# Attention, then a SwiGLU block by fast matrix products: the first block's output product in two passes of two terms each, its last two weight conversions after its up products

## The chip, the cores and the metric

The kernel runs on one core of a Trainium2 chip. The metric is the device time of one execution in microseconds (us), the median of several runs. Engines are named as in the profile: PE (matrix products; PEld is its weight load), DVE (vector engine), ACT (scalar engine), POOL (GpSimd), SP (the queue that issues most transfers).

## The reference

```python
# q, k, v: (8, 12, 448, 64); g_q, g_k: (64,); w_gate, w_val: (768, 1536); w_out: (1536, 768)
def rmsnorm(x, g):
    return x / np.sqrt(np.mean(x * x, axis=-1, keepdims=True) + 1e-06) * g
scores = 1 / np.sqrt(64) * rmsnorm(q, g_q) @ rmsnorm(k, g_k).transpose(0, 1, 3, 2)
attn = softmax(scores)                                 # over the keys
x = (attn @ v).transpose(0, 2, 1, 3).reshape(3584, 768)
g = x @ w_gate
out = (g / (1 + np.exp(-g)) * (x @ w_val)) @ w_out     # (3584, 768)
```

The weights come as 64-bit floating point numbers, everything else as 32-bit ones.

## The kernel before, in words

`general` is a slow version that runs only if a test on `g_q` and `g_k` fails; everything below is `fast`.

**Stages.** Twelve heads make six pairs of heads for each of eight batches, 48 pairs `m`. Two batches make a block of 896 tokens; there are four blocks. The first 12 pairs (`EARLY`) run first. Then, for each block, come its up products (gate and value) and its output products; the 12 pairs of the next block run between the output products.

**Products.** Every matrix product is cut into 3x3 blocks and done with 15 products of sums of blocks. The token sums (`sides`, line 1055) are made on DVE from six raw blocks and stand in `xs` in 15 slots, two of 448 columns each. Up products (`up_product`, L1328) go through four groups `g` of 128 hidden columns, 15 steps, gate and value, two matmuls each, in four banks; a bank is read after each product by ACT (a copy) or DVE (an add or subtract, lines 1272 to 1276). The results, gated, stand in `gt`, six parts of four groups. From them DVE makes token sums again (`combine`, L1454; `combined`, L1049 and L1053), and the output products (`down_product`, L1502) go through 15 steps and two halves `s`. Each adds up four matmuls, one for each group `g`, in bank `s`, which is read before the next step writes it (`DOWN_READ`).

**Weights.** `convert` (L1120) makes 24 sets of weight sums: five transfers load 9 blocks of 64-bit numbers, two ACT instructions, six DVE instructions (shift, sign, round; L1168, L1174, L1180) and twelve POOL instructions (L1199, L1202) follow, and one transfer stores 15 block sums in DRAM, in `up_sides[g]` (16 sets) or `down_sides` (8 sets). `load_sides` brings them back into one of two `ws` buffers, three loads for each group of up products, eight for an output product. The conversions work in places that belong to other tiles: parts of `gt` (`GT`), `hs` (`HS`), the tile of exponentials (`ES`), the slots of `xs` from 6 on (`XS`), the pairs' work tile (`PAIRS`) and `spare` (`SPARE`). `staged[place]` is the last store out of a place; loads of pairs wait for `PAIRS`, scores for `ES`.

**Order.** `Order` (L361) plans all instructions by itself: each piece has a due time `when`, a `rank` that makes it more urgent, a cost in us, what it waits for, and tiles that it takes from rings. At each step it picks, over all engines, the piece that can start earliest, and among those near to each other the one with the smallest `when - rank`. What it emits is the order of each engine's queue. Reads of up banks have rank 60, reads of output banks 20, conversions 20 from the seventh set on. The due times of the conversions are `starts` and `spans`, their places `turns`, at the end of `fast`.

Of the kernel before, what the change touches and what calls it, by code (L numbers as in the profile page):

```python
# [477 lines left out]
def fast(  # L478
# [87 lines left out]
    def take(name, key, shape):  # L566
# [4 lines left out]
        if name in OFTEN:  # L571
            at = OFTEN[name] + order.turn[name] % BUFS[name]
            tiles[name, key] = spare[:, ts(at, S)]
            return tiles[name, key]
        if name == "eh":
            at = order.turn["eh"] % BUFS["eh"]
            tiles[name, key] = more[:, at].rearrange("p (h q) -> p h q", h=2)
            return tiles[name, key]
# [35 lines left out]
    down_sides = dram.tile([P, 15, 2, NG, P], F32, name="down_sides")  # L614
# [88 lines left out]
    def attention(m):  # L703
# [306 lines left out]
        def divide():  # L1010
# [4 lines left out]
            "ACT", 0.55, when + 3.0, copy_sums, after=[last, up_done.get(b // 2 - 1)], uses=at[:1]  # L1015
# [39 lines left out]
    def sides(n, c, when):  # L1055
# [7 lines left out]
        for i, one, two, op in (  # L1063
# [15 lines left out]
            if n == 0:  # L1079
                free = [staged[place] for place in XS]  # L1080
# [39 lines left out]
    def convert(key, src, sums, to, when, place, by_bank):  # L1120

        rank = 20.0 if by_bank else 0.0
# [7 lines left out]
        wait = [last_exp[0]] if place in (ES, PAIRS, GT[2]) else []  # L1130
# [110 lines left out]
    def down_weights(i, *how):  # L1241

        g, s = divmod(i, 2)
        w = moe_w_out.rearrange("(k g p) (n s f) -> p k g n s f", g=NG, p=P, n=3, s=2)
        weights["down", i] = convert(
            ("down", i), lambda k, n: w[:, k, g, n, s], DOWN_SUMS, down_sides[:, :, s, g], *how
        )
# [3 lines left out]
    down_done = {}  # L1251
    last_load = []
# [25 lines left out]
    def load_sides(key, sides, part, sums):  # L1278

        size = 2 * (NC2 if sums is UP_SUMS else NG) * P  # L1280
        to = take(*key, [P, WS])[:, 0 : len(part) * size].rearrange("p (x f) -> p x f", f=size)
        i = 0
        for names, first in ((sums, 0), (BLOCKS, len(sums))):
            here = sorted(names.index(x) for x in part if x in names)
            if here:
                size = len(here)
                src = sides[:, ds(first + here[0], size)]
                nc.sync.dma_start(to[:, ds(i, size)], src.rearrange("p x a b f -> p x (a b f)"))
                i += size
# [5 lines left out]
    def block(n):  # L1295
# [123 lines left out]
        def up_load(g, piece):  # L1419
# [3 lines left out]
                lambda: load_sides(key, up_sides[g], UP_ORDER[5 * piece :][:5], UP_SUMS),  # L1423
# [6 lines left out]
        for g in range(NG):  # L1430
# [5 lines left out]
        up_done[n] = last  # L1436
        bank_read[:] = [free[0, 0], free[0, 1]]
# [3 lines left out]
        raw = [gt[:, :, k] for k in range(6)]  # L1441
        a1, a2, a3, b1, b2, b3 = raw
        h0, h1 = hs[:, 0], hs[:, 1]
# [3 lines left out]
            6: h0, 1: h1, 10: h2, 14: b1, 2: h0, 3: h1, 0: a3, 11: h2, 4: b3, 12: h0, 5: a1, 8: h1,  # L1447
            7: b2, 13: b1, 9: a2,
        }
        all_hidden = [hidden[g, k] for g in range(NG) for k in range(6)]  # L1450
# [3 lines left out]
        def combine(x, one, two, op, when, after, g=None):  # L1454
            to = where[x]
            if g is not None:
                to, one, two = to[:, g], one[:, g], two[:, g]
            done = add(
                "DVE", 0.64 if g is not None else 2.05, when,
                lambda: combined(to, one, two, op), after=after, port=True,  # L1460
            )
            made.setdefault(x, []).append(done)
            return done

        span = (BOTH if n < NB - 1 else DOWN) / 15

        def step_time(x):
            return block_end(n) + DOWN_ORDER.index(x) * span

        for g in range(NG):  # L1470
            when = start + 30 * (g + 1) * unit + 1.0
            before = [down_done.get(n - 1)] + ([staged[HS]] if n == 0 else [])
            combine(6, a1, a2, None, when, [hidden[g, 0], hidden[g, 1], *before], g)
            combine(1, b2, h0, ALU.subtract, when, [made[6][g], hidden[g, 4], *before], g)
        combine(10, h1, b1, None, block_end(n) + 3.0, [*all_hidden, *made[1], up_done[n]])
# [5 lines left out]
        def down_product(step, x, s):  # L1481
            nonlocal last
            when = step_time(x) + s * span / 2
            piece = step // 2
            key = ("ws", (n, "o", piece))
            size = 2 if piece < 7 else 1
            if piece not in loads:
                loads[piece] = add(
                    "SP", 0.9, when - 24.0,
                    lambda: load_sides(key, down_sides, DOWN_ORDER[2 * piece :][:2], DOWN_SUMS),  # L1490
                    after=[*last_load, *(weights["down", i] for i in range(2 * NG))], takes=[key],
                    kb=512 * size, early=10.0,
                )
                last_load[:] = [loads[piece]]
            fresh = x in FRESH

            def emit():
                w = tiles[key][:, 0 : 4 * NG * P]
                w = w.rearrange("p (x s g f) -> p x s g f", s=2, g=NG, f=P)
                at = place_of(x, DOWN_ORDER[step - step % 2 :][:2], DOWN_SUMS)  # L1500
                for g in range(NG):
                    nc.tensor.matmul(  # L1502
                        banks[s][:, 0:S], w[:, at, s, g], where[x][:, g],
                        start=fresh and g == 0, stop=g == NG - 1, skip_group_check=True,
# [3 lines left out]
                "PE", 2 * PRODUCT, when, emit,  # L1508
                after=[
                    last, loads[piece], bank_read[s], *made.get(x, []),  # L1510
# [5 lines left out]
            when += 2 * PRODUCT  # L1516
            t, how, *final = DOWN_READ[x]
            name = "vw"[s] + {"t0": "0", "t1": "1", "t4": "2", "t3": "3", "d": "3", "t5": "4"}[t]
            value = (name, (n, "o", t))
# [15 lines left out]
            if x == 12:  # L1535
                other = ("vw"[s] + "1", (n, "o", "t1"))
# [7 lines left out]
            if not final:  # L1544
# [25 lines left out]
        for step, x in enumerate(DOWN_ORDER):  # L1570
            when = step_time(x)
            for s in range(2):
                down_product(step, x, s)
            after = {
                6: [(2, b3, b1, ALU.subtract, (1,))],
                1: [(3, h0, a3, ALU.add, (2, 10))],
                10: [(11, a3, b3, ALU.add, ()), (4, b2, b3, None, (2, 11))],
                14: [(13, a2, b2, ALU.add, (2, 10))],
                2: [(12, h1, a1, ALU.subtract, (3,))],
                3: [(8, a3, b2, ALU.subtract, (12,)), (9, a2, a3, ALU.add, (6, 13))],  # L1580
            }.get(x, [])
            for to, one, two, op, others in after:
                combine(
                    to, one, two, op, when + span,
                    [*all_hidden, *products[n, x], *(d for o in others for d in made[o])],
                )
# [28 lines left out]
    turns = [(*XS, *GT[:2], HS, SPARE), (ES, PAIRS, GT[2], SPARE, HS), (ES, PAIRS, HS, SPARE), (ES, HS)]  # L1615
    starts = [LEAD - 4.0, FIRST - 20.0, FIRST + 60.0, FIRST + 110.0]
# [81 lines left out]
```

## Time and profile before

| | us |
|---|---|
| median of 3 runs | 1486.81 (1485.77 to 1488.26) |
| profiled execution | 1485.77 |
| its span, first to last instruction | 1484.0 |
| PE busy | 1425.0 |
| DVE busy | 916.0 |
| ACT busy | 681.5 |
| POOL busy | 414.1 |

Stretches of the span, cut where PE goes from one kind of product to the next: first pairs until 141.7; up products of block 0 until 329.7; its output products with pairs 12 to 23 until 505.1; up products of block 1 until 690.6; its output products until 855.3; and so on, with the last output products from 1386.4 on.

The profile is one execution as the hardware recorded it. A matmul stands as two records, so a 128x448 one in groups of x4 is two matmuls. In a timeline, a row is start, length, engine, line, operation, output and input; the bracket at its end is idle time of the engine ahead of it and what ended it. A list of waits has who waited for whom, then us in total, times, and the longest. Idle time of an engine that is off the path costs nothing. The granted PE clock was 0.997 of full speed over the span.

### The profile page before, as it was taken

The numbers are of one execution on the slowest core, as the hardware profiler recorded it, in microseconds if no ns is written. First come the engines' busy times: TensorE is split into PE (matmuls) and PEld (weight loads), VectorE is DVE, ScalarE is ACT, GpSimd is POOL, SyncE is SP. The second block draws the span as 40 slices with busy tenths as digits, with TensorE's granted clock in tenths as the row PEclk, the third lists the DMA queues.
The fourth block names the chain that finished last, engine by engine and source line by source line (L and its number), as shares of the span: only waits on it lengthen the run. The fifth ranks groups of instructions, "written<-read, shape, count | busy, mean of one in ns | idle before, by whom it ended". The sixth has DMA issues, their size and how long they took to land.

```text
span 1484.0 us, 19470 instructions
## 1 busy us (share of the span) xinstructions
PE 1425.0 (96%) x6672; PEld 675.4 (46%) x6672; DVE 916.0 (62%) x1405; ACT 681.5 (46%) x1366; POOL 414.1 (28%) x468
## 2 busy tenths in 40 slices
PE   5789999999999999999999999999999999999998
PEld 2334544443444455544444445554444445555553
DVE  4777887877978544355886733454786854432533
ACT  6774544437775322445767422354676532122100
POOL 2454586636444100012544200011343410000000
PEclk9999999999999999999999999999999999999999
DMA  7767999974453432533344432352353442222235
GB/s 165 158 144 236 292 308 341 296 219 90 99 115 85 113 106 71 138 103 90 74 111 110 100 117 73 106 136 77 96 119 85 90 119 89 80 98 73 83 98 107
DMA packets 415921, 193.30 MB, mean 130 GB/s; under 512 B 324164, under 2 KB 397892, under 8 KB 409668
## 3 DMA queue, kind: packets, MB, share of 16 engines
q1 hardware_dynamic: 402688, 190.35, 48.0%
q10 hardware_dynamic: 12996, 1.61, 0.7%
q8 instruction: 55, 0.90, 0.3%
q14 instruction: 54, 0.44, 0.1%
q0 software_dynamic: 128, 0.00, 0.0%
HBM read 157.29 MB, written 34.60 MB: 129 GB/s over the span
## 4 chain that ended last, share of the span: by engine, by line
PE 73%; DVE 3%; ACT 2%; issue 1%; DMA 1%; SPq 1%; ACTq 0%; DVEq 0%
PE mm L1502 22%; PE mm L1328 20%; PE at L1328 20%; PE st L840 6%; PE at L916 5%; PE st L947 1%; ACT spare L1000 1%; ACT es L855 1%; DVE rd L982 1%; DMA out_dram<-spare 0%; SPq L728 0%; DVE ss L782 0%; DMA work<-in_k_dram 0%; DVE ss L768 0%; DVE sums L866 0%
## 5 line engine op out<-in xcount | busy, mean ns | idle before, releaser
L1328 PE MATMUL mm<-xs,ws 128*128 128x448 f32 x960 | 401.2, 540 | 4.4 <-DVE spare L1276 2.2
L1328 PE MATMUL at<-xs,ws 128*128 128x448 f32 x960 | 400.6, 540 | 4.1 <-DVE v L1274 2.6
L1328 PEld LDWEIGHTS mm<-xs,ws 128*128 128x128 f32 x960 | 181.5, 190 | 185.8 <-issue 173.8
L1328 PEld LDWEIGHTS at<-xs,ws 128*128 128x128 f32 x960 | 181.9, 190 | 184.6 <-issue 172.6
L795 POOL TENSOR_TENSOR work<-work,rr 128x448 f32<-128x448 f32 x96 | 105.9, 1122 | 503.5 <-DVE rr L686 245.2
L840 PE MATMUL st<-work 64*64 64x448 f32 (+1 forms) x1536 | 155.1, 508 | 27.3 <-ACT work L814 21.2
L1502 PE MATMUL mm<-gt,ws 128*128 128x448 f32 x448 | 177.2, 545 | 0.0
L1272 DVE TENSOR_TENSOR gt<-gt,mm 128x448 f32<-128x448 f32 x64 | 39.7, 621 | 185.1 <-PE mm L1328 171.3
L1502 PE MATMUL mm<-hs,ws 128*128 128x448 f32 x384 | 152.1, 545 | 0.9 <-DVE ss L684 0.9
L855 ACT ACTIVATE es<-st 128x896 f32<-128x896 f32 x129 | 114.3, 913 | 56.1 <-PE at L916 42.8
L860 POOL TENSOR_TENSOR sums<-es 128x896 f32<-128x896 f32 x36 | 75.7, 2104 | 195.8 <-PE st L947 83.2
L1402 ACT ACTIVATE st<-gt 128x448 f32<-128x448 f32 x96 | 52.4, 547 | 163.8 <-DVE gt L1276 85.9
L1000 ACT COPY spare<-rd 32x224 f32<-32x224 f32 x288 | 108.1, 375 | 35.0 <-DVE rd L982 30.7
L1502 PEld LDWEIGHTS mm<-gt,ws 128*128 128x128 f32 x448 | 82.9, 190 | 84.2 <-issue 81.0
L916 PE MATMUL at<-es,v 64*64 64x448 f32 x1032 | 110.2, 545 | 7.2 <-ACT xs L1005 3.3
L1270 ACT COPY gt<-mm 128x448 f32<-128x448 f32 x80 | 42.5, 531 | 141.5 <-PE mm L1328 141.4
L1502 PEld LDWEIGHTS mm<-hs,ws 128*128 128x128 f32 x384 | 71.1, 190 | 72.9 <-issue 70.9
L840 PEld LDWEIGHTS st<-work 64*64 64x64 f32 x1536 | 50.9, 134 | 108.7 <-issue 38.1
L1270 ACT COPY v<-at 128x448 f32<-128x448 f32 x96 | 51.1, 532 | 83.2 <-PE at L1328 80.0
L860 POOL TENSOR_TENSOR sums<-sums,es 128x896 f32<-128x896 f32 x36 | 78.7, 2187 | 2.8
L811 DVE STREAM_TRANSPOSE work<-work 128x448 f32<-128x448 f32 x96 | 59.2, 627 | 25.2 <-POOL work L795 23.1
L916 PEld LDWEIGHTS at<-es,v 64*64 64x64 f32 x1032 | 39.7, 134 | 67.4 <-issue 57.4
(150 smaller groups left out, 1568.7 us busy)
## 6 DMA issues: line engine op xcount, KB each, us to landing
ws<-up_sides SPq DMA_DIRECT2D x32, 1024.0 KB, 4.9
ws<-down_sides SPq DMA_DIRECT2D x16, 1024.0 KB, 5.0
ws<-down_sides SPq DMA_DIRECT2D x28, 512.0 KB, 4.0
ws<-up_sides SPq DMA_DIRECT2D x16, 768.0 KB, 4.6
work<-in_q_dram SPq DMA_DIRECT2D x192, 56.0 KB, 2.4
work<-in_k_dram SPq DMA_DIRECT2D x188, 56.0 KB, 2.5
out_dram<-spare SPq DMA_DIRECT2D x168, 56.0 KB, 1.9
v<-in_v_dram SPq DMA_DIRECT2D x96, 96.0 KB, 2.5
```

The costliest lines, as they stand in the source:

```text
L795: nc.gpsimd.tensor_tensor(out=tiles["t", m][:, x], in0=tiles["qk", (m, x)], in1=rr.to_broadcast([P, NC, C]), op=ALU.mult,)
L811: nc.vector.transpose(to, tiles["t", m][:, x].rearrange("p c f -> p (c f)"))
L840: nc.tensor.matmul(st[ds(D * x, D), h, 0:n], tiles["KT", m][rows, ds(P * j + D * of_keys, D)], tiles["QT", m][rows, ds(Q * of_queries, n)] ...
L855: nc.scalar.activation(e, tiles["st", (m, j)][:, :, 0 : S * width(j) // P], AF.Exp)
L860: nc.gpsimd.tensor_tensor(out=to, in0=tiles["e", (m, 0)] if j == 1 else to, in1=e, op=ALU.add)
L916: nc.tensor.matmul(tiles["at", (m, x)][ds(D * h, D), queries], tiles["v", m][rows, j, h], tiles["e", (m, j)][rows, h], start=j == 0, stop= ...
L1000: nc.scalar.copy(inv[ds(D * h + C * to, C), ts(x, Q)], tiles["rd", m][ds(D * h + C * x, C)])
L1270: nc.scalar.copy(to, ps)
L1272: nc.vector.tensor_tensor(out=to, in0=old, in1=ps, op=ALU.add)
L1328: nc.tensor.matmul(ps(), w[:, at, which, c], xs[:, SLOT[x], c], start=fresh and c == 0, stop=c == NC2 - 1, skip_group_check=True,)
L1402: nc.scalar.activation(take(*act, [P, 2, TB])[:, 0, 0:S], to, AF.Silu)
L1502: nc.tensor.matmul(banks[s][:, 0:S], w[:, at, s, g], where[x][:, g], start=fresh and g == 0, stop=g == NG - 1, skip_group_check=True,)
```

## The change

- Block 0's output product runs in two passes. The first takes groups `g` 0 and 1 of all 15 steps, the second groups 2 and 3; each product has two matmuls. Every bank is read once in each pass; in the second pass, values that the first copied are added to or subtracted from, except `d`, whose value of the first pass is kept in a tile of its own (`v5` and `w5`, the latter in a raw slot of `xs`) and subtracted at the end. Sums (`combine`) are made for each pass, half as wide; they follow `BEHIND` and `readers` in place of written lists of waits.
- `down_sides` is two tensors, one for each pair of groups, and a pass's loads wait for its own four conversions; in block 0 a load brings four steps, not two.
- The last two of the 24 conversions go to `XS`, due at the end of the up products and after the last of them. Of the six before, places change: `ES, PAIRS, SPARE, HS, SPARE, HS` in place of `ES, PAIRS, HS, SPARE, ES, PAIRS`.
- All conversions have rank 0.
- Token sums of block 1 wait for the conversions in `XS`, and the copy of pair 23's sums waits for the last use of `w5`.

Other blocks keep one pass. The diff, cut:

```diff
+        if name == "w5":
+            tiles[name, key] = xs[:, SLOT[RAW[1][2]], 1]
+            return tiles[name, key]
...
-    down_sides = dram.tile([P, 15, 2, NG, P], F32, name="down_sides")
+    down_sides = [dram.tile([P, 15, 2, 2, P], F32, name=f"down_sides{i}") for i in range(NG // 2)]
...
-            "ACT", 0.55, when + 3.0, copy_sums, after=[last, up_done.get(b // 2 - 1)], uses=at[:1]
+            "ACT", 0.55, when + 3.0, copy_sums, uses=at[:1],
+            after=[last, up_done.get(b // 2 - 1), *(c3_used if m == 2 * EARLY - 1 else [])],
...
-            if n == 0:
-                free = [staged[place] for place in XS]
+            if n < 2:
+                free = [*free, *(staged[place] for place in XS)]
...
-    def convert(key, src, sums, to, when, place, by_bank):
-        rank = 20.0 if by_bank else 0.0
+    def convert(key, src, sums, to, when, place, by_bank, wait=()):
+        rank = 0.0 if by_bank else 0.0
...
-        wait = [last_exp[0]] if place in (ES, PAIRS, GT[2]) else []
+        wait = [*wait, *([last_exp[0]] if place in (ES, PAIRS, GT[2]) else [])]
...
+        if n == 0:
+            for make, index, when, place in late_weights:
+                make(index, when, place, True, [last])
...
+        passes = [(0, 2), (2, 4)] if n == 0 else [(0, NG)]
...
+        BEHIND = {6: (2,), 1: (3,), 10: (11, 4), 14: (13,), 2: (12,), 3: (8, 9)}
...
-        def combine(x, one, two, op, when, after, g=None):
-            to = where[x]
+        def combine(p, x, when, after, g=None):
+            one, two, op = SUMS[x]
+            names, (to, *values) = zip(*(place(p, i) for i in (x, one, two)))
...
+            us = 0.3 + 0.44 * (passes[p][1] - passes[p][0])
+            if g is None:
+                after += readers.pop(names[0], [])
...
+            many = 4 if n == 0 else 2
+            piece = step // many
...
-                    after=[*last_load, *(weights["down", i] for i in range(2 * NG))], takes=[key],
-                    kb=512 * size, early=10.0,
+                    after=[
+                        *last_load, *(weights["down", g, i] for g in range(lo, hi) for i in range(2))
+                    ],
+                    takes=[key], kb=128 * len(part) * (hi - lo), early=10.0,
...
-                for g in range(NG):
+                for g in range(hi - lo):
...
-                "PE", 2 * PRODUCT, when, emit,
+                "PE", 2 * PRODUCT / len(passes), when, emit,
...
+            sums_too = p and t != "d"
...
+            if split and not p and t == "d":
+                name = "5"
+            value = ("vw"[s] + name, (n, "o", t, 0 if sums_too else p))
+            if sums_too and how == COPY:
+                how = ADD if t in ("t1", "t3") else FROM
...
+                if p:
+                    c3 = ("vw"[s] + "5", (n, "o", "d", 0))
+                    drained[s, "d"] = add(
+                        "DVE", 0.64, when + 1.5,
+                        lambda: nc.vector.tensor_tensor(
+                            out=tiles[value], in0=tiles[value], in1=tiles[c3], op=ALU.subtract
+                        ),
+                        after=[drained[s, "d"]], uses=[value, c3], port=True,
+                    )
+                    c3_used.append(drained[s, "d"])
-            if not final:
+            if not final or p < len(passes) - 1:
                 return
...
+        for p in range(len(passes)):
+            for step, x in enumerate(DOWN_ORDER):
+                for s in range(2):
+                    down_product(p, step, x, s)
+                for other in BEHIND.get(x, ()):
+                    combine(p, other, step_time(p, x) + span, all_hidden)
+                if x == 9 and p < len(passes) - 1:
+                    combine(p + 1, 10, step_time(p, x) + span, all_hidden)
...
-    turns = [(*XS, *GT[:2], HS, SPARE), (ES, PAIRS, GT[2], SPARE, HS), (ES, PAIRS, HS, SPARE), (ES, HS)]
-    starts = [LEAD - 4.0, FIRST - 20.0, FIRST + 60.0, FIRST + 110.0]
-    spans = [13.0, 8.0, 9.0, 10.0]
+    turns = [(*XS, *GT[:2], HS, SPARE), (ES, PAIRS, GT[2], SPARE, HS), (ES, PAIRS, SPARE, HS, SPARE, HS), XS]
+    starts = [LEAD - 4.0, FIRST - 20.0, FIRST + 60.0, block_end(0)]
+    spans = [13.0, 8.0, 9.0, 12.0]
     counts = [6, 10, 6, 2]
...
-            make(index, starts[n] + spans[n] * i, turns[n][i % len(turns[n])], n > 0)
+            when, place = starts[n] + spans[n] * i, turns[n][i % len(turns[n])]
+            if n < 3:
+                make(index, when, place, n > 0)
+            else:
+                late_weights.append((make, index, when, place))
```

## Prediction

> **What bounds the kernel now.** I read the page's busy shares first: PE works 96% of the span, so only idle PE time or work added to PE moves the end. Then busy time by stage, cut where PE passes from one kind of product to the other: up products of block 0, its output products with the second dozen of attention pairs, up products of block 1, output products of blocks 1 and 2.
>
> ```profile
> PE 1425.0 (96%) x6672; PEld 675.4 (46%) x6672; DVE 916.0 (62%) x1405; ACT 681.5 (46%) x1366; POOL 414.1 (28%) x468
> ...
> 141.70:329.70 188.00, 182.28 (x482) 91.10 (x483) 152.37 (x228) 83.19 (x113) 111.84 (x216) 1.00 0.95 293
> 329.70:505.06 175.36, 170.03 (x1105) 71.68 (x1104) 139.10 (x205) 117.74 (x273) 81.27 (x48) 1.00 0.46 102
> 505.06:690.60 185.54, 185.54 (x529) 92.79 (x530) 82.15 (x145) 64.11 (x122) 11.93 (x10) 1.00 0.36 102
> 690.60:855.30 164.70, 162.00 (x1056) 71.65 (x1054) 124.70 (x176) 105.35 (x234) 65.00 (x38) 1.00 0.45 100
> ```
>
> Columns: stretch, length, then busy time of PE, PEld, DVE, ACT and POOL. Block 0 is the exception: its up stage takes 188.0 us though it holds fewer PE instructions than block 1's (185.5 us), and its output stage 175.4 against 164.7. Next, whom PE waits for in block 0's up stage, and PE and DVE in order of time around the longest of these waits:
>
> ```profile
> PE at L1328 <- DVE v L1274: 2.6, 2, 1.5
> PE at L1328 <- DVE v L1272: 1.2, 1, 1.2
> PE mm L1328 <- DMA ws<-up_sides: 0.9, 2, 0.6
> ```
>
> ```profile
> 237.06 1.67 PE L1328 MATMUL mm<-xs,ws 128*128 128x448 f32 x4
> 240.27 1.77 PE L1328 MATMUL at<-xs,ws 128*128 128x448 f32 x4 [1.55 <-DVE v L1274]
> ```
>
> ```profile
> 234.79 0.76 DVE L1168 TENSOR_SCALAR st<-es 128x576 uint32<-128x576 uint32 x1
> 235.64 0.78 DVE L1174 SCALAR_TENSOR_TENSOR st<-es,st 128x576 uint32<-128x576 uint32 x1
> 236.55 0.76 DVE L1180 CUSTOM_DVE_ANT_0 es<-es,st 128x1152 uint16<-128x1152 uint16 x1
> 237.34 0.76 DVE L1168 TENSOR_SCALAR st<-es 128x576 uint32<-128x576 uint32 x1
> 238.14 0.76 DVE L1174 SCALAR_TENSOR_TENSOR st<-es,st 128x576 uint32<-128x576 uint32 x1
> 238.93 0.75 DVE L1180 CUSTOM_DVE_ANT_0 es<-es,st 128x1152 uint16<-128x1152 uint16 x1
> 239.61 0.61 DVE L1274 TENSOR_TENSOR v<-v,at 128x448 f32<-128x448 f32 x1
> ```
>
> The six DVE instructions of one weight conversion stand in a row, 4.8 us, and the bank read behind them comes too late for PE. Other rows of the two timelines show the same run ahead of the waits at 231.9, 268.8, 280.2 and 289.0.
>
> **The PE unit prices.** An up product (four records) starts 1.504 us after the one before; an output product in full is twice that, 3.008. From groups of x16: a 64x448 matmul 0.188, a 64x224 one 0.096. A change of array mode: in block 1's up stage, scores of 1.14 us put between two products move the next one by 1.39 (658.50 to 659.89) and the one after by 0.11 more, 0.35 for two changes, 0.17 each. By these prices the up stage of block 1 is 185.3 (it took 185.5), so they hold.
>
> **Block 0, up stage: removes 6.1 us, takes over 5.5.** From start to start, the five waits on DVE cost 0.66+1.81+1.43+0.92+1.29 = 6.1 (each wait, and 0.1 on the product behind it); the two on `ws` 1.4. In the changed kernel two of the eight output-weight conversions leave this stage, and the rest lose 20 us of rank. I laid its DVE order against its PE order: adding DVE durations between reads, each read due before the fourth product from it starts. For the kernel before this finds four waits, at the products of the last four rows (2.3, 1.1, 0.6, 1.4); for the changed one none, also with all DVE work 10% dearer. So 6.1 goes. The `ws` waits I leave: a lower rank may make stored weights later (up to some 3 us), fewer transfers (DMA share 0.95 here) may remove the 1.4. What comes in: scores of the first pairs, whose places are free earlier, 16 matmuls 64x448 and 8 of 64x224 (3.8 us), with 10 mode changes (1.7). Net -0.6.
>
> **Block 0, output stage: work.** Matmuls are the same 120; pieces are halved, so attention is cut into finer slices: 52 mode changes become 69, +2.9; the moved scores take 3.8 away. Work by prices 167.2 before, 166.4 after: -0.9.
>
> **Block 0, output stage: lost time.** 175.4 - 167.2 = 8.1 before; block 1's has 164.7 - 161.8 = 2.9. The 5.2 between are mostly waits in its first 30 us (PE is idle 3.5 of 330 to 360), where attention starts from nothing because the pairs' and exponentials' tiles were held by conversions until 296 and 316. The changed order starts attention in the up stage as block 1 does, so I take 2.9 as the base. Against that stands DVE. Between the first full sum and the last turned output of block 0 its queue, by durations of this trace, grows from 142.2 to 162.7 us: +32 bank reads and sums of reads (0.62 each, 19.8), +12 conversion instructions (0.757, 9.1), -9.3 of attention moved earlier, +0.9 for sums in halves. From the first DVE read to the last, DVE has 138.5 us to do in 144.3 us of PE work, and a half product gives its bank's read only the other bank's 1.5 us. Laid against each other, PE loses 0.1 us if DVE never waits, 0.7 if its work is stretched by 5%, 6.2 by 11%. DVE does reach 0.91 busy over 40 us (36.46 of 360 to 400), and its waits are mostly for engines it was ahead of, which a later DVE meets no more; I take 2.5. At the end, the last reads now stand ahead of the side sum that block 1's first product needs: two instructions of 0.62 past the last read, +1.3 over the 0.7 wait there now. Loss after: 2.9+2.5+1.3 = 6.7, so -1.4.
>
> **Costed at nothing.** The two late conversions: ACT +5.1 us (118 of 175 busy now), POOL about +14 (81 of 175), covered until the second pass starts some 85 us in. Their loads stand on SP between the first two output-weight loads: 1.15 MB at the 293 GB/s of the up stage is 4 us, the next load lands 5.0 us after its issue, so at about 12 us; PE wants it at 17. Without that cover each late us is one us of PE. The copy of pair 23 that waits for `c3_used` stands a hundred us behind it. The first pass's narrower wait for weights: PE shows no wait on `down_sides`, so nothing gained.
>
> POOL's added instructions meet DVE's sums, and the 448-wide sum at L1053 is 0.667 us here against 0.618 in block 1's up stage, where POOL is almost idle: 0.05 each, under 1 us in all for a sixth more POOL work. [...] Were each of the 24 added POOL instructions (0.46 to 0.52 us) to hold DVE fully, that would be some 12 us more DVE and, by this estimate, a time of up to 1494; the row says otherwise and I stay with it.
>
> **Blocks 1 and 2.** Their output stages are reordered slightly: 42 mode changes become 38 each, -1.4 in all.
>
> **Sum.** -0.6 - 0.9 - 1.4 - 1.4 = -4.3. The profiled execution took 1485.77 (span 1484.0 and 1.8 around it), the lowest of three; it becomes 1481.5. The median is 1.04 higher, so the predicted median is 1482.5.
>
> **Rivals.** *DVE becomes the bound* (slower). The 138.5 us of DVE fill 144.3 plus what PE loses. The break-even is a loss of 2.5+4.3 = 6.8, a DVE 0.917 busy; at 0.89 the loss is 11.3 and the time 1491. At the average fill of this stage now (0.79) it would be 31, far end 1511, but DVE waits then for want of work. For: 0.91 is the best 40 us seen. Against: 380 to 400 has 19.75 of 20.
> *Given back in the output stage* (no change): attention still starts late, the 8.1 stays under the 2.5 and 1.3; 5.2 more, 1487.7.
> *The conversions still stand in the reads' way* (it doesn't do what it says): four runs of six and five of five remain in the changed order; if half the waits stay, 3.0 more, 1485.5.
> *All of it comes*: DVE costs 0.7, the end wait does not grow, the `ws` waits go: -1.8-1.3-1.4, 1478.0.
>
> **How the numbers follow.** About 0.2%, 3.0 us, is what a measurement can tell from no change; faster means under 1483.8. Forecast 0.52 (0.05 of it within 0.2%; its own range 1480 to 1484.5), all of it 0.13, given back and still in the way 0.17 together, DVE bound 0.18. Faster 0.60, within 0.2% 0.22, slower 0.18. The range runs from the full gain, 1478, to a DVE at 0.90 busy, a loss of 9.6 or 7.1 over mine, 1489.6; it leaves out the rest of the DVE case.
>
> **What would show it.** Right: no wait of PE on a bank read over 0.3 us in block 0's up stage, scores within that stage, its length about 187.4 us; the output stage about 173, its DVE over 0.92 busy, PE's waits for DVE reads there below 3 us. Wrong: such waits of over 7 us, waits on `ws` from `up_sides` of several us, or block 1's first products waiting over 4 us on their sums.

## The result and the profile after

The changed kernel takes 1497.61 us (median of 4 runs, 1495.71 to 1500.44) against 1486.29 for the kernel before in runs beside it: ratio 1.0078, 95% interval 1.0056 to 1.0100. It is slower by about 11 us, where 4 us less were forecast. The profiled execution took 1500.44 (span 1498.7), the slowest of the four. Stage lengths, here and below, are those of one profiled execution of each kernel.

The page's busy shares of the changed kernel: PE is again at 96%, of a longer span.

```profile
PE 1439.1 (96%) x6672; PEld 679.1 (45%) x6672; DVE 935.3 (62%) x1446; ACT 694.6 (46%) x1378; POOL 411.4 (27%) x468
```

Busy time by stage, cut as before: up products of block 0, its output products, up products of block 1, output products of blocks 1 and 2. Columns: stretch, length, busy PE, PEld, DVE, ACT, POOL, granted clock, DMA share, GB/s.

```profile
143.10:331.78 188.68, 187.32 (x533) 92.65 (x533) 152.13 (x232) 100.53 (x146) 107.23 (x200) 1.00 0.93 283
331.78:523.56 191.78, 176.80 (x1057) 72.42 (x1055) 159.62 (x235) 114.06 (x249) 84.53 (x66) 0.97 0.42 100
523.56:710.06 186.50, 185.88 (x529) 92.43 (x529) 87.31 (x154) 66.58 (x129) 11.93 (x10) 1.00 0.39 106
710.06:872.56 162.50, 161.20 (x1058) 72.18 (x1056) 122.14 (x176) 105.16 (x234) 64.58 (x38) 1.00 0.46 102
```

From first product to first product, before and after:

| stage | before | after | measured | forecast |
|---|---|---|---|---|
| start of the up products of block 0 | 140.13 | 143.10 | +3.0 | 0 |
| up products, block 0 | 189.58 | 188.68 | -0.9 | -0.6 |
| output products, block 0 | 175.35 | 191.78 | +16.4 | -2.3 |
| up products, block 1 | 185.34 | 186.50 | +1.2 | 0 |
| output products, blocks 1 and 2 | 164.90, 165.04 | 162.50, 162.45 | -5.0 | -1.4 |

(The prediction cut block 0's up stage 1.57 us later, hence its 188.0.) The start moves between kernels that are alike up to there (140.1 in the kernel before, 143.2 in the one with gaps in block 3, below; 139.0 to 143.2 in all) and isn't the change's. So the loss is in one stage, and there the granted clock is 0.97, not 1.00. PE is idle 15.0 us of it (191.78 - 176.80) against 5.3 before: +9.7; a stretch of half clock, shown below, costs about 5; some 2 remain. The up stage did what was forecast: no wait for a bank read is left in it, scores stand in it.

For whom PE waits in that stage (us in total, times, longest), after:

```profile
PE at L920 <- DVE xs L1012: 6.5, 3, 3.7
PE mm L1551 <- ACT v L1277: 3.7, 2, 2.7
PE st L844 <- ACT es L859: 2.0, 3, 1.6
PE mm L1337 <- DVE spare L1283: 1.2, 1, 1.2
PE st L844 <- DVE gt L1414: 0.9, 1, 0.9
```

Lines have moved: L920 is the matmul that weighs the values by exponentials, L1012 the join on DVE that empties its bank, L844 the scores, L1551 and L1337 the output and up products, L1277 ACT's copy of an output bank. DVE's reads of output banks, the only reads that my count of lags had followed, are not in the list, up to the 1.2 at the end. DVE is late all the same: for the attention's bank. DVE in order of time ahead of the longest wait, then PE:

```profile
348.88 1.08 DVE L1054 SCALAR_TENSOR_TENSOR gt<-gt 128x896 f32<-128x896 f32 x1
349.88 0.75 DVE L1173 TENSOR_SCALAR st<-xs 128x576 uint32<-128x576 uint32 x1
350.67 0.76 DVE L1179 SCALAR_TENSOR_TENSOR st<-xs,st 128x576 uint32<-128x576 uint32 x1
351.47 0.75 DVE L1185 CUSTOM_DVE_ANT_0 xs<-xs,st 128x1152 uint16<-128x1152 uint16 x1
352.26 0.76 DVE L1173 TENSOR_SCALAR st<-xs 128x576 uint32<-128x576 uint32 x1
353.05 0.76 DVE L1179 SCALAR_TENSOR_TENSOR st<-xs,st 128x576 uint32<-128x576 uint32 x1
353.85 0.75 DVE L1185 CUSTOM_DVE_ANT_0 xs<-xs,st 128x1152 uint16<-128x1152 uint16 x1
354.52 0.61 DVE L1012 TENSOR_TENSOR xs<-xs,at 128x448 f32<-128x448 f32 x1
```

```profile
350.66 0.93 PE L920 MATMUL at<-es,v 64*64 64x448 f32 x4
355.28 4.00 PE L920 MATMUL at<-es,v 64*64 64x448 f32 x18 [3.69 <-DVE xs L1012]
...
360.70 3.35 PE L1551 MATMUL mm<-hs,ws 128*128 128x448 f32 x4
```

It is the picture that the change took out of the up stage: six instructions of one conversion in a row, and behind them what PE needs. The conversion's input is `xs`: it is one of the two that were moved here. And the products behind the wait are slow: four records of an output product last 3.35, where 1.77 is usual. The same kernel by short stretches (columns as above) tells why:

```profile
350.90:354.30 3.40, 0.69 (x4) 0.00 (x0) 3.26 (x5) 3.31 (x9) 2.80 (x3) 0.99 0.84 273
354.30:364.50 10.20, 9.22 (x36) 3.42 (x40) 1.24 (x3) 2.30 (x4) 6.03 (x12) 0.50 0.16 40
```

After 3.4 us with 0.7 of PE work the granted clock is 0.50 for 10.2 us. The stall costs 3.7 idle and about 5 more (half of the 9.22 us that PE works in this stretch is 4.6; by PE's busy time, 176.80 here and 171.52 in the kernel less both parts below, whose clock stays full in this stage, it is 5.3). Shorter gaps than this one have half clock behind them too, in other kernels here (1.76 and 1.98 us, last section).

### The profile page after: what moved, and what is told of

Its sections match the earlier page's. It is cut to its first block, busy times and chain, and to the rows that moved or that the text cites. A ratio compares the mean times of both kernels' runs of the same rounds, so it can differ in the third digit from the quotient of the medians.

```text
span 1498.7 us, 19540 instructions
## 1 busy us (share of the span) xinstructions
PE 1439.1 (96%) x6672; PEld 679.1 (45%) x6672; DVE 935.3 (62%) x1446; ACT 694.6 (46%) x1378; POOL 411.4 (27%) x468
## 4 chain that ended last, share of the span: by engine, by line
PE 83%; DVE 5%; DMA 3%; SPq 3%; ACT 2%; issue 1%; POOL 0%; DVEq 0%; ACTq 0%; POOLq 0%
PE at L1337 23%; PE mm L1337 23%; PE mm L1551 22%; PE at L920 7%; PE st L844 7%; PE st L951 1%; SPq L732 1%; DMA out_dram<-spare 1%; ACT es L859 1%; DVE rd L986 1%; SPq L1141 1%; DVE work L815 0%; DMA ws<-up_sides 0%; PE mm L951 0%; DVE xs L1058 0%
## 5 line engine op out<-in xcount | busy, mean ns | idle before, releaser
L1337 PE MATMUL mm<-xs,ws 128*128 128x448 f32 x960 | 401.5, 540 | 3.9 <-DVE spare L1283 2.7
L1337 PE MATMUL at<-xs,ws 128*128 128x448 f32 x960 | 400.6, 540 | 0.6 <-ACT v L1277 0.6
L1337 PEld LDWEIGHTS mm<-xs,ws 128*128 128x128 f32 x960 | 181.4, 190 | 185.6 <-issue 173.4
L1337 PEld LDWEIGHTS at<-xs,ws 128*128 128x128 f32 x960 | 181.8, 190 | 180.7 <-issue 172.4
L844 PE MATMUL st<-work 64*64 64x448 f32 (+1 forms) x1536 | 159.9, 514 | 27.4 <-ACT work L818 21.6
L1551 PE MATMUL mm<-gt,ws 128*128 128x448 f32 x448 | 177.7, 545 | 0.0
L1551 PE MATMUL mm<-hs,ws 128*128 128x448 f32 x384 | 155.0, 551 | 2.7 <-ACT v L1277 2.7
L920 PE MATMUL at<-es,v 64*64 64x448 f32 x1032 | 118.8, 561 | 11.9 <-DVE xs L1012 8.5
L1551 PEld LDWEIGHTS mm<-gt,ws 128*128 128x128 f32 x448 | 82.8, 190 | 83.9 <-issue 77.4
L1277 ACT COPY gt<-mm 128x448 f32<-128x448 f32 x80 | 42.6, 533 | 138.8 <-PE mm L1337 138.6
L1551 PEld LDWEIGHTS mm<-hs,ws 128*128 128x128 f32 x384 | 71.1, 191 | 76.4 <-issue 69.6
L844 PEld LDWEIGHTS st<-work 64*64 64x64 f32 x1536 | 52.0, 135 | 111.0 <-issue 37.1
L1277 ACT COPY v<-at 128x448 f32<-128x448 f32 x96 | 51.1, 532 | 79.9 <-PE at L1337 76.4
L864 POOL TENSOR_TENSOR sums<-sums,es 128x896 f32<-128x896 f32 x36 | 77.8, 2162 | 11.4 <-ACT es L859 8.7
L920 PEld LDWEIGHTS at<-es,v 64*64 64x64 f32 x1032 | 41.9, 137 | 76.2 <-issue 64.9
```

Source lines behind the costliest of these rows:

```text
L844: nc.tensor.matmul(st[ds(D * x, D), h, 0:n], tiles["KT", m][rows, ds(P * j + D * of_keys, D)], tiles["QT", m][rows, ds(Q * of_queries, n)] ...
L864: nc.gpsimd.tensor_tensor(out=to, in0=tiles["e", (m, 0)] if j == 1 else to, in1=e, op=ALU.add)
L920: nc.tensor.matmul(tiles["at", (m, x)][ds(D * h, D), queries], tiles["v", m][rows, j, h], tiles["e", (m, j)][rows, h], start=j == 0, stop= ...
L1277: nc.scalar.copy(to, ps)
L1337: nc.tensor.matmul(ps(), w[:, at, which, c], xs[:, SLOT[x], c], start=fresh and c == 0, stop=c == NC2 - 1, skip_group_check=True,)
L1551: nc.tensor.matmul(banks[s][:, 0:S], w[:, at, s, g % 2], side[:, g], start=fresh and g == 0, stop=g == hi - lo - 1, skip_group_check=True,)
```

## Experiments

The first theory: the two late conversions stand on DVE ahead of joins, and the stall halves the clock. The rivals: it isn't their place but DVE's total work that is too much; POOL's additions slow DVE; the two passes cost by themselves. And which part of the change is worth anything?

### Late conversions due 30 us later

```diff
-    starts = [LEAD - 4.0, FIRST - 20.0, FIRST + 60.0, block_end(0)]
+    starts = [LEAD - 4.0, FIRST - 20.0, FIRST + 60.0, block_end(0) + 30.0]
```

> The two passes as changed, only the two late weight conversions due 30 us later. Theory 'late join': in the changed kernel the six DVE instructions of the first late conversion (4.7 us) stand ahead of the join at L1012, which frees a bank of the weighted sums; PE idles 3.7 us there and then runs at half clock for 10 us (about 4.8 us lost). With the joins ahead of the conversion there is no idle stretch of PE over 2.5 us and no half clock in block 0's output stage, that stage takes 176 to 182 us (191.8 in the changed kernel), and the time is 1486 to 1491. Rival 'DVE too full': its DVE queue holds the same 162.7 us in that stage, so the same loss turns up at other reads: 1494 to 1500.

1501.87 us, ratio 1.0106 (1.0089 to 1.0123), above what either theory expected; the output stage takes 190.4. PE's longest waits in it:

```profile
381.65 3.67 PE L920 MATMUL at<-es,v 64*64 64x448 f32 x18 [3.43 <-DVE xs L1012]
401.42 3.53 PE L920 MATMUL at<-es,v 64*64 64x448 f32 x18 [3.76 <-DVE xs L1012]
```

The planner put both conversions ahead of two later joins; each wait halved the clock for 3.4 us. The premise, that no conversion stands ahead of a join, wasn't met: the run says only that the stall moves with the conversions.

### The two late conversions left out

```diff
-                make(index, when, place, True, [last])
+                pass
```

with group 2's sums stored a second time for group 3.

> The two passes as changed, but the two late conversions are left out: the sums of output weights of group 3 are those of group 2, stored a second time. DVE's queue in block 0's output stage loses 9.1 us of conversions, POOL's about 14. 'Late join': output stage 168 to 174 us, time 1484 to 1489, because the passes by themselves cost no more than 17 mode changes. 'DVE too full': DVE still has 153 us beside 162 of PE work; output stage over 178 us, time 1492 to 1497. A third reading, that POOL's conversions hold up DVE's sums, expects this kernel fast and the one with later conversions still slow.

1489.20 us, ratio 1.0014 (1.0005 to 1.0024): 8.4 of 11.3 us gone. The planner found another order (up stage 195.8, output stage 175.4, together 371.1 against 364.9 before and 380.5 after), so this shows how much goes with the conversions, not by which engine; the stage lies between what the two theories expected.

### Each half of a late conversion behind a join

```diff
+                if when >= block_end(0) and x == 0:
+                    late_steps.append(last)
...
+    for i, step in enumerate(late_steps):
+        step["after"].append(joins[EARLY + i])
```

> The changed kernel, with each half of the two late conversions (three DVE instructions, 2.3 us) made to wait for a join (L1012 in the changed kernel): of pairs 12, 13, 14 and 15 in turn, so that none stands just ahead of a join. The kernel with conversions 30 us later did not test this: its planner put them ahead of the next two joins again, and PE idled 3.4 and 3.8 us there. 'Late join': no idle time of PE over 2 us ahead of a weighted sum in the first 60 us of block 0's output stage and no half clock there; the stage 178 to 185 us (191.8 in the changed kernel), time 1486 to 1492. 'DVE too full': as much DVE work in the same stage, the loss turns up elsewhere, 1495 or more.

1503.55 us, ratio 1.0112 (1.0096 to 1.0127). No weighted sum waits for a join in the first 60 us of the output stage, as wanted; the stage still takes 192.7 and block 1's up stage 190.6, and later:

```profile
392.14 2.03 PE L1556 MATMUL mm<-hs,ws 128*128 128x448 f32 x4 [2.42 <-DVE w L1288]
418.64 1.01 PE L920 MATMUL at<-es,v 64*64 64x448 f32 x2 [3.04 <-DVE xs L1012]
450.78 0.98 PE L844 MATMUL st<-work 64*64 64x448 f32 x8 [1.53 <-ACT es L859]
496.10 3.68 PE L920 MATMUL at<-es,v 64*64 64x448 f32 x18 [4.49 <-DVE xs L1012]
```

The first of these is a wait for a DVE read of an output bank, the kind that the prediction did count; the clock is half for 3.4 us behind it. So one unlucky place is not the cause. The place is the form that the loss takes.

### The places of the change, one pass

The kernel before with rank 0 and places `ES, PAIRS, SPARE, HS, SPARE, HS`, then `SPARE, HS`:

```diff
-    turns = [..., (ES, PAIRS, HS, SPARE), (ES, HS)]
+    turns = [..., (ES, PAIRS, SPARE, HS, SPARE, HS), (SPARE, HS)]
```

> The kernel before with the change's places and rank alone: one pass, all conversions in the up stage, the last six of them in SPARE and HS in turn, so that the tiles of pairs and exponentials are free early; all conversions at rank 0. Both theories blame the output stage for the loss and expect the gain that was forecast without the loss: no runs of conversions ahead of reads (6 us) and attention started early (5 us): 1476 to 1481. If the early start of attention is worth nothing, 1481 to 1485; if conversions in two places alternately become late for the output weights, over 1487.

1505.72 us, ratio 1.0130 (1.0113 to 1.0147). The scores' tiles are free early, so attention starts in the up stage (232.8 us, and 150.5 for the output stage), among conversions:

```profile
345.80 0.97 PE L947 MATMUL st<-sums,many 128*32 128x224 f32 x8 [8.08 <-DVE hs L1180]
...
371.15 2.52 PE L916 MATMUL at<-es,v 64*64 64x448 f32 x12 [8.35 <-DVE xs L1008]
```

The same neighbours, PE's attention and DVE's conversions, collide without passes too. Around each of these two waits the clock is half for 13.7 us (340.25 to 353.90 and 360.73 to 374.38), in part while PE is idle.

### Two passes, all conversions in the up stage

```diff
-    ... (ES, PAIRS, SPARE, HS, SPARE, HS), XS]
+    ... (ES, PAIRS, SPARE, HS, SPARE, HS), (ES, HS)]
```

with the due time of the last two back at `FIRST + 110.0`, with no wait for the last up product.

> Two passes as changed, but the last two conversions in the up stage, in ES and HS as before, so that no conversion is left in the output stage. The order now puts the scores and the first weighted sums of two pairs (53 matmuls more than in the changed kernel) into the up stage, among conversions. If only conversions in the output stage cost time, 1483 to 1488. If any weighted sum that PE meets while conversions run makes it idle for over 3 us and lose its clock, as in the kernel with one pass and new places (8.1 and 8.4 us of idle time, 27 us at half clock), 1493 or more.

1512.43 us, ratio 1.0177 (1.0161 to 1.0192). Waits of 3.87 for a conversion, 2.44 and 7.50 for sums and a join behind one, and half clock of 13.7 us twice, all in the up stage; two stretches of 3.4 us at half clock in the output stage; a triple of 1.05, 1.55 and 1.76 us stands in the second pass as in the changed kernel (at 476.84, 483.69 and 498.19 there). Up and output stage together take 396.4 us, against 383.2 in the one-pass kernel above, where one of the last two conversions has another place (`SPARE`, not `ES`): with two passes and the sums' rule it is 13.2 more.

### The same order, less the late conversions' POOL or DVE instructions

In the next three the planner still places and costs every piece, so that each engine's order is the changed kernel's to the instruction, in the traces too; only some emit nothing. They separate what leaving the conversions out could not.

```diff
-            last = add("POOL", us, when, op, after=[last], port=True)
+            last = add(
+                "POOL", us, when, (lambda: None) if late else op, after=[last], port=True
+            )
```

> The changed kernel with the same order on every engine, but the 24 POOL additions of the two late conversions are left out (their sets of weight sums hold other numbers, so group 3's part of the output is not the reference's). If DVE's twelve late conversion instructions ahead of joins are the cause, the idle time of PE ahead of the weighted sum some 20 us into block 0's output stage stays at 3 us or more with its half clock, and the time stays at 1495 or above (output stage at least 188 us). [...]

```diff
-                    "DVE", ..., when, lambda k=k, op=op: op(k),
+                    "DVE", ..., when, lambda k=k, op=op: None if late else op(k),
```

> The changed kernel with the same order on every engine, but the twelve DVE instructions of the two late conversions are left out (shift, sign and rounding of the last two sets of weights are not done). If those twelve are the cause, the idle time ahead of the weighted sum some 20 us into the output stage falls below 1 us, there is no half clock there, and the time is 1491 or below (output stage 182 or less). [...]

Both edits:

> The changed kernel with the same order on every engine, but both the twelve DVE instructions and the 24 POOL additions of the two late conversions are left out; loads, the two ACT instructions of each and the stores stay. What is left over the kernel before is then the price of the two passes themselves, minus the sums' rule. If the late conversions were all of the loss, 1484 or below. If the passes have a price of their own (more bank reads and half sums on DVE), as the kernel with the conversions left out suggested, 1486 to 1490, with PE's late waits for DVE reads from 150 us into the stage on still there.

| kernel | median us | ratio (95%) | output stage | DVE busy in it |
|---|---|---|---|---|
| changed | 1497.61 | 1.0078 (1.0056 to 1.0100) | 191.78 | 159.62 |
| less POOL's 24 | 1496.27 | 1.0067 (1.0047 to 1.0086) | 189.60 | 156.75 |
| less DVE's 12 | 1490.08 | 1.0028 (1.0017 to 1.0038) | 184.30 | 150.01 |
| less both | 1487.30 | 1.0012 (0.9996 to 1.0027) | 180.70 | 147.97 |

PE's waits of over 1 us in the stage's first 100 us, less POOL's additions (those after it are shown for the last kernel only):

```profile
353.80 4.00 PE L920 MATMUL at<-es,v 64*64 64x448 f32 x18 [3.69 <-DVE xs L1012]
372.59 1.72 PE L920 MATMUL at<-es,v 64*64 64x448 f32 x12 [1.13 <-DVE xs L1012]
```

Less DVE's steps:

```profile
385.31 4.97 PE L1553 MATMUL mm<-hs,ws 128*128 128x448 f32 x8 [2.73 <-ACT v L1279]
```

Less both, the whole stage:

```profile
361.24 1.34 PE L920 MATMUL at<-es,v 64*64 64x448 f32 x10 [1.21 <-DVE xs L1012]
...
461.88 1.77 PE L1555 MATMUL mm<-xs,ws 128*128 128x448 f32 x4 [1.05 <-ACT v L1281]
468.73 0.98 PE L844 MATMUL st<-work 64*64 64x448 f32 x8 [1.55 <-ACT es L859]
483.24 2.10 PE L920 MATMUL at<-es,v 64*64 64x448 f32 x18 [1.76 <-DVE xs L1012]
508.54 2.07 PE L1341 MATMUL mm<-xs,ws 128*128 128x448 f32 x4 [1.16 <-DVE spare L1287]
```

Without the twelve DVE instructions the 3.69 and its half clock are gone: 7.5 us of the stage. With them, and without POOL's additions, 3.69 stays to the hundredth, so POOL does not make that stall. But 2.2 us of the stage go with POOL's part, and 3.6 where DVE's is gone too. Of the 3.6, only 0.8 is idle time. The other 2.8 is PE busy for longer (174.32 against 171.52) because of two stretches of half clock, and the second of them follows a wait of 1.76 us that the kernel less both has as well, at full clock: about half of the 2.8 is chance. By the medians POOL's part is 1.3 and 2.8 us, and the intervals overlap. So the waits show that POOL's part costs PE time; how much it costs is not settled. Theirs is the 2.66 wait on ACT's copy at 396.68 in the changed kernel; the 2.73 here is the same one. DVE, POOL and ACT around it, changed kernel:

```profile
388.63 0.81 DVE L689 SCALAR_TENSOR_TENSOR ss<-ss,rr 128x28 f32<-128x28 f32 x1
389.48 2.00 DVE L690 SCALAR_TENSOR_TENSOR rr<-ss,rr 128x28 f32<-128x28 f32 x1
391.40 1.54 DVE L986 RECIPROCAL rd<-st 128x224 f32<-128x224 f32 x1
```

```profile
389.36 2.07 POOL L864 TENSOR_TENSOR sums<-es 128x896 f32<-128x896 f32 x1
391.51 2.08 POOL L864 TENSOR_TENSOR sums<-sums,es 128x896 f32<-128x896 f32 x1
```

```profile
392.98 3.09 ACT L1004 COPY spare<-rd 32x224 f32<-32x224 f32 x8 [5.18 <-DVE rd L986]
396.09 0.53 ACT L1277 COPY v<-mm 128x448 f32<-128x448 f32 x1
```

L690, of 128x28 numbers, usually takes 0.19 us; here it lasts until POOL's 2.07 us sum ends. The reciprocal behind it is late, ACT's eight copies wait for it, and behind them on ACT's queue stands the copy that frees PE's bank. Less POOL's additions L690 takes 0.19 at this place and the wait isn't there: the late additions had pushed POOL's sums of exponentials onto these small instructions. (In that kernel the sums come earlier and meet others, L786 with 1.53 us for one, and PE shows no wait on ACT's copy there. The kernel before has such a meeting too, 1.96 us for L686 at 393.48 beside a POOL sum of 2.13 us, but there the reciprocal stood ahead of it and PE waited for nothing.)

Less both, the stage still takes 5.4 us more than before. DVE's busy time is 8.9 above that of before (147.97 against 139.09), and the last four waits listed above, 5.5 us, stand in the changed kernel too, equal to within 0.06; in the kernel before only the last of them is there, at 0.72.

### The sums' rule alone, and with rank 0

The change without passes, places and due times: what is left is `BEHIND` and `readers` (and two tensors for `down_sides`, and planned costs of sums that differ by at most 0.02 us).

```diff
-        passes = [(0, 2), (2, 4)] if n == 0 else [(0, NG)]
+        passes = [(0, NG)]
```

> The change without its passes and without its new plan of conversions (one pass in every block, ranks, places and due times as before): what is left is the new rule for the sums of the output product (they wait for the readers of what they overwrite, through a list) and output weights in two tensors. In the changed kernel the output stages of blocks 1 and 2 took 162.45 us, before 164.9 and 165.0. If the new rule for the sums did that, block 0's stage gains too: 2.5 us in each of three, 1477.5 to 1482. If it came from elsewhere, 1485 to 1488.

1483.57 us, ratio 0.9976 (0.9967 to 0.9986): faster than both kernels. The output stages of blocks 1 and 2 take 162.45 and 162.46, as in the changed kernel; block 0's takes 1.4 more than before (176.76). In block 1's output stage of the kernel before, one wait is

```profile
774.96 3.27 PE L1502 MATMUL mm<-xs,ws 128*128 128x448 f32 x8 [1.37 <-ACT spare L1270]
```

and it is absent now; PE is busy 161.2 us in place of 162.2. These are the 2.45 us, twice.

The second kernel has rank 0 for all conversions besides.

```diff
-        rank = 20.0 if by_bank else 0.0
+        rank = 0.0
```

> The one before, and all conversions at rank 0. If the rank keeps runs of six conversion instructions from standing ahead of bank reads (waits of 6 us in block 0's up stage before), the up stage falls from 189.6 to 183.5 and the time to 1472 to 1477, as nothing else moves into that stage. If conversions become late instead, they hold up the start of the output stage and the pairs: at least what is gained, 1478 to 1486.

1484.73 us, ratio 0.9987 (0.9978 to 0.9996). The up stage gains 1.2 us over the sums' rule alone and still has a 1.47 us wait for a read; behind it the later conversions cost more than that:

```profile
328.62 6.30 PE L1551 MATMUL mm<-hs,ws 128*128 128x448 f32 x8 [3.21 <-DMA ws<-down_sides]
...
337.32 3.23 PE L844 MATMUL st<-work 64*64 64x224 f32 x24 [2.40 <-ACT work L818]
```

### Gaps made on purpose

The kernel before, with 8, 10, 12 and 14 more DVE instructions ahead of one bank read in each group of block 3's up stage, where nothing else runs.

```diff
+            if n == NB - 1 and step == 5 and which:
+                for i in range((8, 10, 12, 14)[g]):
+                    slow = add("DVE", 0.7, when + 0.2, ..., after=[slow], rank=60.0)
+                before = [slow]
```

> The kernel before, with 8, 10, 12 and 14 extra DVE instructions (they write a tile that is no longer used) ahead of one bank read in each of the four groups of block 3's up stage, where nothing else runs: PE should idle there about 1.8, 3.2, 4.6 and 6.0 us. If idle stretches make the clock drop, the longer two or three are followed by some 7 to 10 us at clock 0.5, 3.4 to 5 us lost each, and the time is 1511 to 1518; if the half clock in the changed kernel had another cause, the clock stays 1.00 there and the time is 1501 to 1503.

One run, 1502.3 us, which was expected if the clock stayed full. It did not, but the gaps came out smaller than meant:

```profile
1231.82 1.77 PE L1328 MATMUL at<-xs,ws 128*128 128x448 f32 x4 [0.38 <-DVE v L1272]
1278.90 1.77 PE L1328 MATMUL at<-xs,ws 128*128 128x448 f32 x4 [1.71 <-DVE v L1272]
1327.29 3.36 PE L1328 MATMUL at<-xs,ws 128*128 128x448 f32 x4 [3.03 <-DVE v L1272]
1378.61 3.31 PE L1328 MATMUL at<-xs,ws 128*128 128x448 f32 x4 [4.35 <-DVE v L1272]
```

Behind 0.38 and 1.71 the product is as fast as ever (1.77). Behind 3.03 and 4.35 it takes twice as long, the clock is half for 3.4 us, and the next one is normal.

## Why the prediction was wrong

**Up stage of block 0: right.** -0.6 forecast, -0.9 measured, all five waits for bank reads gone.

**Work of the output stage: off by 2.4 us.** The prices said -0.9. PE's busy time less both parts of the late conversions, where the clock is full, is 171.52 against 170.02, so 1.5 more. DVE's growth came out as forecast, 20.5 (142.2 to 162.7; measured 139.10 to 159.62), but in part by luck: 2.9 of it is POOL's doing (point 3 below), and less both parts the growth is 8.9, where the forecast less the twelve conversion instructions has 11.4.

**The step that failed is the output stage's lost time,** "2.9+2.5+1.3 = 6.7, so -1.4". Measured by the same prices it is 191.8 - 166.4 = 25.4, with the 2.4 of work in it. Three things in it:

1. The 2.5 for a full DVE came from laying DVE's reads of output banks against the products that need the banks. PE needs more of DVE than these: the join that frees the attention's bank, the reciprocal that ACT waits for ahead of its own bank copies. DVE's total was right, and DVE was late for readers that I had not listed. Taking the twelve instructions out is worth 7.5 us of the stage. Those twelve were counted, 9.1 us of DVE time, but with no place: "costed at nothing" named cover for ACT, POOL and the loads of the late conversions, never for the six in a row on DVE, which is what I had just removed from the stage before.
2. Lost time was idle time only. With one gap of 3.69 us came 10.2 us at half clock, about another 5.
3. POOL's additions were given under 1 us, from a sum that took 0.667 in place of 0.618. DVE's busy time is 2.9 us higher with them than without (159.62 against 156.75), and the stage 2.2 us longer (3.6 without DVE's twelve, part of that chance). The case that I worked out and put aside, each added POOL instruction holding DVE fully, gave 12 us, four times too many (and should have been 13, as six of the 24 additions take 0.73 to 0.80 us). What the trace shows is one L690 of 2.00 us that ends at 391.48, where POOL's sum ends at 391.43; whether POOL's instructions hold DVE in general was not shown. A mean over a stage had hidden it: nine of the ten L690 in this stage take 0.19 us, one takes 2.00.

**The end wait: half right.** +1.3 forecast for the start of block 1; the wait there is 1.22 in place of 0.72, 0.5 more. Block 1's up stage, forecast unchanged, takes 1.2 more.

**Blocks 1 and 2: too small.** -1.4 forecast for both, -5.0 measured. Mode changes were counted, and PE's busy time in block 1's did fall by 1.0; the wait of 1.37 that the new order of sums removes wasn't looked for.

**The rival** "DVE becomes the bound" named the right place and side, from 1491 up to a far end of 1511; the measured time lies between. What spoke against it, 19.75 of 20 us busy at one place, says what DVE can do when nobody waits for a particular instruction, and no more. But its mechanism, a DVE without time left, is not what came: DVE is busy 0.83 of the stage (159.62 of 191.78 us). Nor did any of the prediction's signs of being wrong appear: PE's waits for DVE reads are 1.2 us in that stage, where over 7 was the sign. They watched the same readers as the count of lags.

**The account.** Over the whole change, by the profiled executions and without the moving start, the parts are: late conversions 11.1 us of the stage, 10.3 by the medians (7.5 to 8.9 DVE's steps, 2.2 to 3.6 POOL's sums, taken with or without the other), the two passes with the rest of the conversions (ACT's instructions, loads, stores) 3.9 in the stage over the sums' rule in one pass and 1.2 behind it, the sums' rule -5.0 in blocks 1 and 2 and +1.4 in block 0, the up stage -0.9: 11.7 in all, where the medians differ by 11.3; single executions of one kernel lie up to 8 us apart, so that the two agree so well is luck. How the 3.9 divides between half sums, extra bank reads and those remains of the conversions was not separated. Nor is it a fixed price: up and output stage together, it is 3.5 here, and 13.2 lie between the two kernels with all conversions in the up stage. Nor was it tried to place the late additions so that POOL's sums do not meet L690.

## What to carry to other kernels

An engine can be late for somebody while it has time left, as DVE at 0.83 of this stage: list everyone who waits for it (banks of every kind, and engines whose own queue then holds back a bank), not only the readers that the change is about, and lay the moved block of work at its new place against that list. Price a stall with the slow clock that may come with it. And test the parts of a change alone: the 5 us that the sums' rule brings in blocks 1 and 2 (3 us in all, by its own run) were hidden under 16 that the rest cost.

## What the hardware showed

The length of a gap alone does not decide whether the clock is halved. The same wait of 1.76 us ahead of the same matmuls is followed by half clock in the kernel less DVE's steps:

```profile
484.79:488.20 3.41, 1.65 (x10) 0.43 (x12) 3.41 (x7) 0.67 (x1) 0.00 (x0) 1.00 0.01 2
488.20:491.61 3.41, 3.41 (x21) 1.32 (x18) 2.22 (x3) 0.00 (x0) 0.00 (x0) 0.50 0.00 0
```

and by full clock in the changed kernel:

```profile
494.21:497.62 3.41, 2.23 (x8) 0.57 (x6) 3.38 (x7) 0.57 (x1) 0.00 (x0) 1.00 0.00 0
497.62:501.04 3.42, 2.85 (x32) 1.51 (x34) 2.99 (x4) 0.09 (x1) 0.00 (x0) 1.00 0.00 0
```

Nor did the 2.66 at 396.68 halve it, where the 2.73 of its sister run did. All stretches of half clock in these traces ahead of the kernel's end are 3.41 us or a multiple of it: twice 6.83 and once 10.24 in the changed kernel.

They lie on a grid. Within a run, all stretches of half clock start a whole number of 3.413 us apart, to 0.003 us (74.37, 98.26 and 354.26 in the changed kernel: 7 and 75 steps; 340.25 and 360.73 in the one-pass kernel with the change's places: 6). With a window for one step of this grid, the traces differ in how much PE works within one window, by the profile's busy time. In all thirteen kernels, from 130 us to 8 us before the end, 21 windows at full clock have 1.65 us of PE work or less, and each is followed by half clock; none with 1.66 or more is. The 2.73 lies whole in one window, with 0.69 of work left. The 2.66 is split by an edge (2.20 and 1.96 of work in the two windows), and so is the 1.76 of the changed kernel, above. The 1.98 with half clock behind it in the kernel with conversions behind joins (at 525.91) lies whole in a window with 1.43 of work. A wait of 1.76 that lies whole in a window leaves 1.65 of work (less DVE's steps, above, with half clock behind it) or 1.66; less POOL's additions the clock stayed full:

```profile
492.46:495.88 3.42, 1.66 (x18) 0.74 (x19) 3.42 (x6) 0.67 (x1) 0.00 (x0) 1.00 0.00 0
495.88:499.29 3.41, 3.41 (x31) 1.62 (x23) 1.13 (x3) 1.36 (x3) 0.00 (x0) 1.00 0.00 0
```

Busy time is not all of it: in the first 130 us, with attention alone, a window with 1.59 us of work (kernel before, from 70.24) and one with 1.65 (changed kernel, from 12.93) have full clock behind them. How long the half clock lasts stays open. It was one window after gaps of 3.43, 3.76 and 4.49 us with the attention's small matmuls behind them and three after 3.69 with the same; with full 128x128 products behind, one after 3.03 and 4.35 and two after 3.21.
